# A bias moved ahead of the first values, a late normalization, earlier transposes, and more zero matmuls at the start of a sliding-window attention and gated MLP kernel

## The chip, the cores and the metric

The kernel runs on one core of a Trainium2 chip. The metric is the device time of one execution in microseconds (us). Each execution also lists its span (first to last instruction; here always 1.7 to 1.8 us less than the time) and the mean granted clock of TensorE, the share of full speed that the profiler recorded. At a mean clock of 0.998 or more, the executions of the kernel before lay between 342.41 and 343.31 us, so they agree within 0.3%.

Engine names in the profile: PE is TensorE, PEld its weight loads, DVE is VectorE, ACT is ScalarE, POOL is GpSimd, SP is SyncE.

## The reference

```python
# shortened
def _attn_ref(q, k, v):            # q, k, v: (8, 8, 576, 64), float32
    scores = scale * q @ k^T
    mask = (rel >= 0) & (rel < 64) # causal, window of 64
    attn = softmax(where(mask, scores, -1e9))
    return attn @ v

def _moe_ref(x, w_gate, w_val, w_out):   # x: (4608, 512), d_ff 1536
    return (maximum(x @ w_gate, 0) * (x @ w_val)) @ w_out
# the attention output, heads joined, is x
```

## The kernel before

The attention is cut in 24 units of 192 query rows with all 8 heads. Two units fill one tile of 384 rows, on which the MLP works. A unit goes through: scores (`u_st`, PE, into "st" in PSUM, where the kernel keeps all its matmul results: "st", "pv", "h", "op"), exp (`u_exp`, ACT, "p"), for units from 2 on a multiplication with the band mask (`u_mask`, DVE), values and row sums (`u_pv`, PE, "pv"), copy of the values (`u_copy`, ACT, "xv"), 32x32 transposes of the sums (`u_sum`, DVE, "sT"), reciprocal and transpose back (`u_back`, DVE, "rT", "rs"), product (`u_norm`, DVE, "xt"). Units 0 and 1 have no mask multiplication: a bias of 0 or -30000 is laid into PSUM by matmuls with the identity (`u_bias`) and the scores add to it.

The MLP's hidden layer makes, for 128 of the 1536 columns at a time, a gate product and a value product "h" on PE, a relu on ACT ("r_sb") and a product on DVE ("g_sb", called a gate below). Then the output matmuls "op" run over g_sb.

All this is woven into one order of instructions by a program clock: `W.at(t, fn)` puts `fn` into the order at program time `t`. Moving a number moves an instruction in the order of its engine, and adds no work.

```python
    def heat(n, to, start=True):
        for _ in range(n):
            nc.tensor.matmul(to, zero[:, 0:128], zero[:, 0:to.shape[1]], ...)   # adds zeros
    ...
    def plan_batch(b, load, trans):          # one batch: transposes of k (2), q (2) at times trans
        ...
    def plan_unit(u, T, exp=0.8, mask=1.5, pv=3.9, copy=(4.7, 6.0), norm=(4.8, 6.1, 7.4, 8.7), gap=0.6):
        W.at(T, lambda: u_st(u))
        ...                                   # v_load; u_exp and u_mask, group by group; u_copy
        W.at(T + pv, lambda: u_pv(u))
        for t, fn in zip(norm, (lambda: u_sum(u, 1), lambda: u_sum(u, 0), lambda: u_back(u), lambda: u_norm(u))):
            W.at(T + t, fn)
    ...
        plan_batch(1, None, (37.5, 39.0, 40.4, 41.8))
    ...
        W.at(5.3, lambda: u_bias(0))
        W.at(5.4, lambda: heat(10, units[0]["spare"], False))
        W.at(8.7, lambda: u_st(0, (0,)))
        W.at(9.5, lambda: heat(8, units[0]["spare"], False))
        W.at(11.0, lambda: u_st(0, (1,)))
        ...                                   # exps and copies of unit 0, exps of unit 1
        W.at(11.4, lambda: u_pv(0, (0, 1)))
        W.at(11.45, lambda: u_bias(1, (2, 3)))
        W.at(11.5, lambda: u_pv(0, (2, 3)))
        W.at(11.6, lambda: u_bias(1, (0, 1)))
        W.at(11.7, lambda: u_st(1))
    ...
        fast = 0.8, 1.5, 3.9, (4.1, 5.3), (4.2, 5.4, 6.4, 7.5), 0.5
        plan_unit(2, 24.0, *fast)
        plan_unit(3, 42.5, *fast)
    ...
        W.advance(13.7)
        ready(1)
        hidden(0, 0, U, 0, 4, 4)              # tile 0, rows of unit 0, first 4 column blocks
        ready(2)
        hidden(0, U, TT, 0, 4, 4)             # rows of unit 1
        hidden(0, 0, TT, 4, NF, 4)            # all rows, the other 8 blocks
        output_by_rows(0)
        ready(3)
        hidden(1, 0, U)                       # tile 1 begins
```

The softmax here doesn't subtract the row's maximum and nothing guards it: scores larger than these inputs give would overflow.

## Time and profile before

| | before |
|---|---|
| time, median of 3 | 342.76 us (342.64 to 342.87) |
| the profiled execution | time 344.84 us, span 343.1 us, mean clock 0.995 |
| PE busy | 332.7 us, 97% of the span |
| DVE, ACT busy | 251.5 us, 186.7 us |

The page's line of busy time by engine:

```profile
PE 332.7 (97%) x2950; PEld 201.2 (59%) x2950; DVE 251.5 (73%) x452; ACT 186.7 (54%) x383; POOL 65.7 (19%) x99
```

With PE at 97% the question is where the other 10 us lie. The prediction shows the rest of the profile before. How its lines are read: in a timeline, the first number is the start in us, the second the time until the group's last instruction ended, then engine, source line, operation, out<-in, shapes and count; in brackets stands how long the engine had been idle before and what ended that idle time. In a table by windows, PE's busy time is the first number after the window's length, and the granted clock stands third from the end. The prediction's stalls are measured from start to start, which gives more than the recorded idle time (1.33 us against 0.76 at the end of tile 0).

The prediction's replay leans on one more thing in this profile: ACT's copies of unit 0's values and DVE's transposes of its sums, which both read "pv", take turns. The copies start at 13.04 us, after 0.42 us for the transposes, and at 15.02; the next transposes at 15.37, behind that copy; the last copy at 16.05, after 0.71 us for them.

### The profile page before, as it was taken

The page shows a single profiled execution, that of the slowest core. Times are in us where ns is not written, and L with a number is a line of the kernel's source. Part 1 is how long each engine was busy: PE and PEld are TensorE (multiplying, and loading weights), DVE is VectorE, ACT ScalarE, POOL GpSimd, SP SyncE. Part 2 cuts the span into 40 slices and gives each one's busy share as a digit, 9 for nine tenths or more (in the row PEclk, how much of TensorE's full clock was granted, in tenths as well). Part 3 has the DMA queues.
Part 4 walks back from the last instruction along what each step waited for, and adds up shares of the span by engine and source line. Part 5 has one row for each costly group of instructions (what it writes and reads, how often), then busy time and mean ns, then how long its engine had stood idle before and what let it go on. Part 6 is the DMA issues. An engine that isn't in the chain of part 4 may idle for free.

```text
span 343.1 us, 7364 instructions
## 1 busy us (share of the span) xinstructions
PE 332.7 (97%) x2950; PEld 201.2 (59%) x2950; DVE 251.5 (73%) x452; ACT 186.7 (54%) x383; POOL 65.7 (19%) x99
## 2 busy tenths in 40 slices
PE   8789999999999999999999999999999999999996
PEld 4476477956646556555555655654664664664653
DVE  5587948998898775797888873878968974875430
ACT  4547157645737546556565565564664663763322
POOL 8723421420122211220120410420120200000000
PEclk9899999999999999999999999999999999999999
DMA  8999998790361941961352962874306401001002
GB/s 214 176 206 196 201 167 150 87 178 31 25 84 42 166 58 63 158 74 63 23 48 77 116 80 92 89 100 105 25 5 119 33 2 71 22 2 62 31 2 93
DMA packets 59666, 30.29 MB, mean 88 GB/s; under 512 B 46064, under 2 KB 51056, under 8 KB 59632
## 3 DMA queue, kind: packets, MB, share of 16 engines
q0 software_dynamic: 53872, 19.21, 52.4%
q1 hardware_dynamic: 5616, 10.55, 8.3%
q8 instruction: 23, 0.38, 0.4%
q14 instruction: 11, 0.09, 0.1%
q10 hardware_dynamic: 144, 0.07, 0.1%
HBM read 39.58 MB, written 9.44 MB: 143 GB/s over the span
## 4 chain that ended last, share of the span: by engine, by line
PE 80%; DVE 11%; issue 4%; DMA 2%; POOL 1%; ACT 1%; ACTq 0%; DVEq 0%; POOLq 0%
PE h L412 48%; PE op L426 21%; PE pv L305 6%; DVE sT L335 3%; PE st L246 3%; DVE g_sb L400 2%; DMA v<-in_v_dram 2%; DVE qT L184 2%; DVE xt L350 1%; DVE rs L344 1%; DVE p L266 1%; DVE kT L184 1%; PE op L458 1%; PE pv L287 1%; PE st L206 1%
## 5 line engine op out<-in xcount | busy, mean ns | idle before, releaser
L400 DVE TENSOR_TENSOR g_sb<-r_sb,h 128x384 f16<-128x384 f32 x144 | 78.3, 549 | 54.0 <-PE h L412 45.8
L412 PE MATMUL h<-xt,wg 128*128 128x384 f16 (+1 forms) x640 | 116.5, 310 | 0.7 <-DVE xt L350 0.7
L412 PE MATMUL h<-xt,wv 128*128 128x384 f16 (+1 forms) x640 | 116.6, 310 | 0.2 <-ACT r_sb L397 0.2
L397 ACT ACTIVATE r_sb<-h 128x384 f32<-128x384 f32 x144 | 71.2, 496 | 51.3 <-PE h L412 43.1
L426 PE MATMUL op<-wo,g_sb 128*128 128x512 f16 x420 | 93.3, 379 | 0.5 <-DVE g_sb L400 0.5
L412 PEld LDWEIGHTS <-wg 128*128 128x128 f16 x640 | 59.3, 98 | 34.7 <-DVE xt L350 1.4
L412 PEld LDWEIGHTS <-wv 128*128 128x128 f16 x640 | 59.7, 98 | 32.0 <-issue 0.5
L192 POOL DMA_DIRECT2D v<-in_v_dram x48 | 40.4, 846 | 189.5 <-PE pv L305 170.1
L426 PEld LDWEIGHTS <-g_sb 128*128 128x128 f16 x420 | 40.9, 98 | 48.8 <-issue 1.1
L335 DVE STREAM_TRANSPOSE sT<-pv 64x384 f32<-64x384 f32 x88 | 51.1, 580 | 11.4 <-PE pv L305 9.8
L260 ACT ACTIVATE p<-st 128x512 f16<-128x512 f32 x92 | 49.9, 604 | 11.6 <-PE st L246 11.4
L433 ACT COPY o_sb<-op 128x512 f32<-128x512 f32 x35 | 20.5, 586 | 61.1 <-PE op L426 61.0
L323 ACT COPY xv<-pv 64x384 f32<-64x384 f32 x88 | 41.7, 474 | 18.3 <-DVE sT L335 8.5
L266 DVE TENSOR_TENSOR p<-p,mask 128x512 f16<-128x512 f16 x88 | 34.2, 420 | 6.5 <-ACT p L260 5.9
L305 PE MATMUL pv<-p,v 128*128 128x128 f16 x352 | 24.1, 219 | 0.4 <-DVE p L266 0.4
L344 DVE STREAM_TRANSPOSE rs<-rT 128x768 f32<-128x768 f32 x24 | 23.5, 979 | 0.8
L305 PEld LDWEIGHTS <-v 128*128 128x128 f16 x352 | 21.6, 98 | 3.7 <-issue 0.9
L350 DVE TENSOR_TENSOR xt<-xv,rs 128x768 f16<-128x768 f32 x24 | 22.7, 947 | 0.7
L184 DVE STREAM_TRANSPOSE kT<-k 128x576 f32<-128x576 f32 (+1 forms) x18 | 19.8, 1119 | 1.9 <-ACT k L177 1.8
L184 DVE STREAM_TRANSPOSE qT<-q 128x576 f32<-128x576 f32 x16 | 19.0, 1239 | 0.9 <-DMA q<-in_q_dram 0.8
L246 PE MATMUL st<-qT,kT 32*128 32x128 f16 x768 | 16.1, 215 | 2.2 <-DVE qT L184 2.2
L246 PEld LDWEIGHTS <-kT 32*128 32x128 f16 x768 | 11.5, 92 | 10.5 <-issue 10.5
(46 smaller groups left out, 80.3 us busy)
## 6 DMA issues: line engine op xcount, KB each, us to landing
out_dram<-o_sb SPq DMA_DIRECT2D x35, 256.0 KB, 2.0
v<-in_v_dram POOLq DMA_DIRECT2D x38, 128.0 KB, 4.0
q<-in_q_dram POOLq DMA_DIRECT2D x16, 288.0 KB, 8.3
k<-in_k_dram POOLq DMA_DIRECT2D x14, 288.0 KB, 6.4
wg<-in_moe_w_gate_dram POOLq DMA_DIRECT2D x3, 512.0 KB, 11.2
wv<-in_moe_w_val_dram POOLq DMA_DIRECT2D x3, 512.0 KB, 13.0
wo<-in_moe_w_out_dram POOLq DMA_DIRECT2D x3, 512.0 KB, 16.3
k<-in_k_dram SPq DMA_DIRECT2D x2, 576.0 KB, 4.0
```

What stands on the lines that cost most here:

```text
L184: nc.vector.transpose(dst.rearrange("p (i j) -> p j i", i=32)[:, j0:j1], src[:, j0:j1])
L192: nc.gpsimd.dma_start(v16[p0:128, w, :, 0:64], v[b, :, k0 + p0:k0 + 128].rearrange("h p d -> p h d"))
L246: nc.tensor.matmul(d["st"][hh][g][:, c:c + 128], kT[rows, hh, ks + 128 * w:ks + 128 * w + 128, dh], qT[rows, hh, ks + 64 * w:ks + 64 * w + ...
L260: nc.scalar.activation(d["p"][g].rearrange("p h c -> p (h c)"), d["st"][0][g], ACT.Exp, scale=scale)
L266: nc.vector.tensor_tensor(p, p, mask.rearrange("p w c -> p (w c)")[:, None, :].to_broadcast([128, 2, 256]), MUL)
L305: nc.tensor.matmul(d["pv"][c % 2][:, c // 2, e, 64 * w:64 * w + 128], v16[:, w, 128 * h - 64 * e:128 * h - 64 * e + 128], d["p"][h % G][:, ...
L323: nc.scalar.copy(d["xs"][rows, n::2], d["pv"][n][rows, :, e, 0:U])
L335: nc.vector.transpose(to[64 * e:64 * e + 64, half::2], d["pv"][half][64 - 64 * e:128 - 64 * e, :, e, 0:U])
L397: nc.scalar.activation(part(r_sb), part(h1), ACT.Relu)
L400: nc.vector.tensor_tensor(g_sb[:, f:f + w, c0:c1], part(r_sb), part(h2), MUL)
L412: nc.tensor.matmul(h[:, b * n:b * n + n], wt[:, c, (f + b) * 128:(f + b) * 128 + 128], xt[:, c, c0:c1], start=(c == 0), stop=(c == NC - 1))
L426: nc.tensor.matmul(op, g_sb[:, f, bass.ds(sub * 128, 128)], wo[:, f], start=(f == 0), stop=(f == NF - 1))
```

## The change

Three things are intended. At the start, PE should not stand idle while it waits for the q transpose and the v transfer: four more zero matmuls, and the first half of unit 1's bias before the values. At the end of tile 0, the gates should not stand in DVE's order behind unit 2's normalization. And the last q transpose of batch 1 should not stand behind the first gate of tile 1.

```diff
-        plan_batch(1, None, (37.5, 39.0, 40.4, 41.8))
+        plan_batch(1, None, (37.0, 37.8, 39.4, 40.8))
...
-        W.at(5.4, lambda: heat(10, units[0]["spare"], False))
+        W.at(5.4, lambda: heat(11, units[0]["spare"], False))
...
-        W.at(9.5, lambda: heat(8, units[0]["spare"], False))
+        W.at(9.5, lambda: heat(11, units[0]["spare"], False))
...
-        W.at(11.45, lambda: u_bias(1, (2, 3)))
+        W.at(11.35, lambda: u_bias(1, (2, 3)))
...
-        plan_unit(2, 24.0, *fast)
+        plan_unit(2, 23.0, 0.8, 1.5, 3.9, (4.7, 6.0), (4.8, 7.4, 11.2, 11.3), 0.6)
```

## The prediction

> **What bounds the kernel now.** I read the page first: TensorE (PE) is busy for 332.7 us of a 343.1 us span, so only some 10 us can be gained anywhere by reordering, and 2% (6.9 us) would take two thirds of that. The chain of waits says the same (80% of it is PE). So I asked where PE is not working, with the busy time by stage. The windows are cut at the places where the records of the granted clock change (5.32, 12.15, 15.56 us) and at the starts of the blocks of matmuls.
>
> ```profile
> 5.32:8.74 3.42, 3.01 (x37) 2.17 (x35) 2.62 (x5) 1.52 (x3) 3.42 (x5) 1.00 1.30 186
> 8.74:12.15 3.41, 1.83 (x43) 1.21 (x33) 2.06 (x3) 1.95 (x7) 3.06 (x5) 1.00 2.72 134
> 12.15:15.56 3.41, 3.41 (x34) 1.71 (x34) 1.36 (x4) 1.43 (x5) 2.31 (x3) 0.50 1.24 203
> 15.56:18.97 3.41, 2.17 (x65) 1.68 (x64) 3.23 (x7) 2.38 (x5) 1.27 (x2) 1.00 1.24 206
> ...
> 24.96:37.32 12.36, 12.13 (x114) 7.54 (x113) 9.59 (x22) 7.84 (x16) 4.07 (x6) 1.00 1.36 201
> 37.32:45.94 8.62, 8.09 (x38) 3.51 (x36) 6.32 (x8) 1.17 (x2) 4.63 (x7) 1.00 2.30 168
> 45.94:49.81 3.87, 3.50 (x66) 3.10 (x64) 2.11 (x3) 1.57 (x3) 0.17 (x1) 1.00 2.39 159
> ```
>
> The columns are the window, its length, busy time of PE, weight loads, VectorE (DVE), ScalarE (ACT), GpSimd, then the granted clock, DMA share and GB/s. See row three: PE is busy without a gap, but at a granted clock of 0.50. The window before it had PE busy for 1.83 of 3.41 us (54%); the one after had 2.17 (64%) and the clock was not lowered after it. After 75 us PE has no stage of this size left: 99.80 of 100 us between 100 and 200, and again between 200 and 300. Everything is decided before 50 us. There the timeline of PE shows what it waits for:
>
> ```profile
> 8.86 1.05 PE L213 MATMUL st<-zero 128*128 128x256 f16 x8
> 10.97 0.41 PE L246 MATMUL st<-qT,kT 32*128 32x128 f16 x16 [1.06 <-DVE qT L184]
> 11.31 0.25 PE L287 MATMUL pv<-p,v 128*64 128x128 f16 x2
> 12.08 0.29 PE L287 MATMUL pv<-p,v 128*64 128x128 f16 x2 [0.52 <-DMA v<-in_v_dram]
> ...
> 12.95 1.03 PE L206 MATMUL st<-bias,ident 128*128 128x512 f16 x2
> 13.91 0.42 PE L287 MATMUL pv<-p,v 128*64 128x128 f16 x4
> ```
>
> Two holes, 1.06 us before the second scores and 0.52 us before the values, make the 54%. The bias of unit 1 (0.96 us at half clock, 12.95 to 13.91) stands between the two halves of unit 0's values. Later, at the end of tile 0:
>
> ```profile
> 36.67 0.81 PE L412 MATMUL h<-xt,wv 128*128 128x384 f16 x4 [0.23 <-ACT r_sb L397]
> 38.57 1.02 PE L426 MATMUL op<-wo,g_sb 128*128 128x512 f16 x4 [0.22 <-DVE g_sb L400]
> 38.44 0.94 DVE L350 TENSOR_TENSOR xt<-xv,rs 128x768 f16<-128x768 f32 x1
> 39.30 1.01 DVE L400 TENSOR_TENSOR g_sb<-r_sb,h 128x384 f16<-128x384 f32 x2
> ```
>
> The gates (g_sb) that free PSUM for the output wait on DVE behind unit 2's four transposes, reciprocal, transpose back and normalization.
>
> [...]
>
> **The change part by part.** The built order shows one more zero matmul before the first scores, three more before the second, the bias pair of unit 1 before unit 0's values, scores of unit 2 four matmuls earlier and its values four matmuls earlier, and on DVE the reciprocal, transpose and normalization of unit 2 after the last gate of tile 0. From the transposes of batch 1 on only their place against the first gate of tile 1 differs.
>
> *Zeros.* Four of about 0.11 us[...]. The first hole (0.41 us) and the second (1.06 us) hold them: no cost on the path. The second hole shrinks to some 0.74 us.
>
> *Bias.* Two matmuls of 512 columns, 0.43 us at full clock, go into the 0.52 us before the v transfer lands (12.04 us in the trace). Then that hole is about 0.1 us. PE in 8.74 to 12.15 is busy 1.83 + 0.32 + 0.42 = 2.57 us, 75%[...]. So I expect full clock from 12.15.
>
> *First stage, replayed.* v lands as before, 12.08. Values of channels 0 and 1 end their issue at 12.47 instead of 12.80 (0.11 instead of 0.21 us per four). The exps end at 12.62, so the second half of the values starts at 12.68 (before: 13.91) and has channel 2 by about 13.1. ACT copies channels 0 and 1 from 12.9 to 13.6[...], channel 2 13.63 to 13.95, DVE transposes two to 14.63, ACT copies channel 3 to 14.98. The exps of unit 1 then start at 15.04 instead of 16.43: **1.39 us earlier**. PE's bias and scores (to 14.2) are no longer on this path, ACT is. From there to the first matmul of tile 0 (19.08 before) all durations stay: 17.69. Weights landed at 15.54, 18.17, 20.76, 23.29, 25.80, 28.80 us; they are used at 17.7, 19.0, 23.6, 26.2, 29.4, 32.9, so none becomes a wait.
>
> *End of tile 0.* From 24.96 to 45.94 are 20.98 us. Work by start-to-start spacing: 64 matmuls of 384 columns at 0.1625 = 10.40, scores 0.57, values 0.90, 36 output matmuls at 0.216 = 7.78: 19.65. Stalls 1.33 us (recorded idle 0.76[...]). Replayed with the new DVE order, the gates 8 to 11 end at about 34.3, 36.0, 36.4, 36.9 against outputs that ask for them at 35.5, 36.3, 37.2: **1.33 us gained**. Unit 2's xt is done by about 39.2, tile 1 asks for it at 43.2. Its values start at 30.65, v landed 29.95: it fits.
>
> *Scores of unit 3.* They stood 0.49 us (48.97 expected, 49.46 seen) for the last q transpose, which stood on DVE behind the first gate of tile 1, at 47.68. Now it comes before that gate; q landed at 43.41, transposed by 44.8, scores at about 46: **0.49 us gained**.
>
> Sum: 1.39 + 1.33 + 0.49 = 3.2 us; 342.76 − 3.2 = 339.6.
>
> **The rivals.** (1) *The clock falls one window later.* With PE faster and ACT the bound, PE stands from about 14.25 to 15.6; in 12.15 to 15.56 it is busy only some 2.1 us[...]. Then 15.56 to 18.97 runs at half, and the first 1.28 us of tile 0 before 18.97 do half their work, a loss of some 0.65 plus 0.2 in the values: 340.4. I give it two in five. (2) *The clock falls as before*[...]. The moved bias still lets the second half of the values start at 12.95, but bias and scores of unit 1 run at half until 15.75: exps at 15.85, gain 0.6 in place of 1.39: 340.4 too. One in six. (3) *A transfer becomes the bound*: slack is 0.7 us for v of unit 2, 0.8 for the second weights and 1.1 for q of batch 1; each could return some 0.3 us. (4) *The delayed normalization makes tile 1 wait*: 4 us of slack speak against it. (5) *DVE bound at 60 to 70 us* (busy 98%) gives time back: its order there is unchanged and follows PE, so hardly.
>
> **Range and chances.** Between 339.6 (all three gains) and 340.4 (a clock rival), I say 339.9. [...]three runs before lay within 0.23 us; gains mis-sized by half a microsecond each give 339.0 to 341.2. To be faster by over 2% it would have to lie under 335.9: the 6.9 us are more than PE's whole idle time from 5 to 60 us (5.0, by the busy times of windows of 5 us) and half of the half-clock stretch (1.7) together; to be slower, over 349.6, of which there is no sign. So within 2%, 0.98.
>
> **What would show it.** Right: clock 1.00 from 12.15 to 15.56; bias at about 11.3 and second values at about 12.7; exps of unit 1 at 15.0; first tile-0 matmul at 17.7; no wait of outputs for gates and none of relu before 37 us; scores of unit 3 without a wait; the first matmul of tile 1 about 2.7 us earlier; from 60 us on a constant offset of about 3.2. Wrong: a row at 0.50 clock anywhere after 12 us; a DMA named as releaser of PE at tile 0; more recorded PE idle between 20 and 60 us than the 1.8 of before (40 less 38.19).

## The result

The changed kernel took 340.80 us (median of 4, 340.72 to 340.91) against 342.75 us (342.64 to 342.87), beside each other. The ratio is 0.9943, with a 95% interval of 0.9926 to 0.9960. A ratio is the mean time of one kernel's executions over that of the other's of the same rounds, so it is not quite the ratio of the medians. By this the kernel is 1.95 us faster, which is within 2%, and the time lies in the predicted range.

The profiled execution after spans 339.0 us, its mean clock is 0.999. That is 4.1 us less than the profiled execution before, but the times differ by 1.95 us only. One of the two profiles does not stand for the timed executions.

PE's timeline of the changed kernel, the start and the end of tile 0:

```profile
10.64 0.41 PE L246 MATMUL st<-qT,kT 32*128 32x128 f16 x16
10.99 0.61 PE L206 MATMUL st<-bias,ident 128*128 128x512 f16 x2
11.53 0.30 PE L287 MATMUL pv<-p,v 128*64 128x128 f16 x4
...
14.79 0.22 PE L287 MATMUL pv<-p,v 128*64 128x128 f16 x1 [0.93 <-ACT p L260]
...
16.80 1.49 PE L412 MATMUL h<-xt,wg 128*128 128x192 f16 x16
...
34.64 7.93 PE L426 MATMUL op<-wo,g_sb 128*128 128x512 f16 x36
...
45.15 0.64 PE L246 MATMUL st<-qT,kT 32*128 32x128 f16 x32
...
55.67 0.83 PE L412 MATMUL h<-xt,wg 128*128 128x192 f16 x8 [0.26 <-DVE xt L350]
```

Two lines of DVE and one of ACT from the same execution:

```profile
14.13 2.07 ACT L260 ACTIVATE p<-st 128x512 f16<-128x512 f32 x4
...
34.75 1.48 DVE L400 TENSOR_TENSOR g_sb<-r_sb,h 128x384 f16<-128x384 f32 x3
...
37.50 0.96 DVE L350 TENSOR_TENSOR xt<-xv,rs 128x768 f16<-128x768 f32 x1
```

The hole before the second scores is gone, and the bias fills the wait for v. The 36 output matmuls run in one row without a wait, and the 32 score matmuls of unit 3 in one row too; the last three gates of tile 0 now come before unit 2's product on DVE. One hole has grown: PE stands 0.93 us before the values of unit 1, for ACT's exps (0.69 us in the first profile). The same in the table by windows, cut at the starts of the stages:

```profile
22.67:34.64 11.97, 11.97 (x114) 7.54 (x113) 8.97 (x20) 7.83 (x16) 3.73 (x6) 1.00 1.37 200
34.64:42.41 7.77, 7.77 (x38) 3.52 (x36) 7.26 (x10) 1.17 (x2) 4.02 (x5) 1.00 1.29 202
42.41:45.72 3.31, 3.31 (x66) 3.05 (x64) 2.30 (x4) 1.57 (x3) 1.45 (x4) 1.00 3.74 125
```

PE is busy through all three: 11.97 of 11.97 us, 7.77 of 7.77, 3.31 of 3.31. Before, these stages were 12.36, 8.62 and 3.87 us long. That is 0.39, 0.85 and 0.56 us less, 1.80 us in sum.

### The profile page after: what moved, and what is told of

Same layout as the page of the kernel before. It is cut to its first block, busy times and chain, and to the rows that moved or that the text cites. A ratio compares the mean times of both kernels' runs of the same rounds, so it can differ in the third digit from the quotient of the medians.

```text
span 339.0 us, 7368 instructions
## 1 busy us (share of the span) xinstructions
PE 331.4 (98%) x2954; PEld 201.0 (59%) x2954; DVE 251.9 (74%) x452; ACT 186.1 (55%) x383; POOL 65.6 (19%) x99
## 4 chain that ended last, share of the span: by engine, by line
PE 85%; DVE 10%; issue 3%; ACT 1%; ACTq 0%
PE h L412 50%; PE op L426 21%; PE pv L305 6%; PE st L246 3%; DVE sT L335 3%; PE st L213 2%; DVE g_sb L400 2%; DVE qT L184 1%; DVE xt L350 1%; DVE p L266 1%; DVE kT L184 1%; PE op L458 1%; ACT p L260 1%; DVE rs L344 1%; PE st L206 1%
```

## The experiments

**Theory A**: the half-clock stretch from 12.15 to 15.56 us, on which the first step of the prediction rests, belongs to that one profiled execution. In the timed executions before, PE had its full clock, the start is bounded by ACT's copies and exps, and the gain is the end of tile 0 and the scores of unit 3. **Rival B**: the stretch belongs to each execution of the kernel before, and the start gave most of the gain. There were twelve runs, all correct, in three calls of four, each in five rounds beside the kernel before. Two calls ran on chip 13 and the middle one on chip 8, so a run is compared with the kernel before of its own call.

### The kernel before, again

No edit.

> The kernel before, unchanged, to see its granted clock in the timed executions. Theory A (the half-clock window of the first profile is an accident of that one execution, and the timed ones ran at full clock): spans near 341.0 us, mean clock 0.999 or more in nearly all executions, time 342.75. Rival B (the window at half clock belongs to every execution of this kernel): spans near 343.1 us at a mean clock of 0.995.

Measured: 342.75 us median of 6. Five of them have spans of 340.8 to 341.1 us at a mean clock of 1.000; one has 342.8 us at 0.994. All eleven executions of the kernel before in the same call have 0.999 or 1.000. Theory A holds on the clock, and B falls. This profile fell in a usual execution. PE's timeline of it, and ACT's exps of unit 1:

```profile
10.78 0.41 PE L246 MATMUL st<-qT,kT 32*128 32x128 f16 x16 [0.52 <-DVE qT L184]
11.12 0.33 PE L287 MATMUL pv<-p,v 128*64 128x128 f16 x4
...
11.71 0.61 PE L206 MATMUL st<-bias,ident 128*128 128x512 f16 x2
12.25 0.30 PE L287 MATMUL pv<-p,v 128*64 128x128 f16 x4
...
14.18 2.07 ACT L260 ACTIVATE p<-st 128x512 f16<-128x512 f32 x4
...
14.83 0.22 PE L287 MATMUL pv<-p,v 128*64 128x128 f16 x1 [0.83 <-ACT p L260]
...
16.84 1.49 PE L412 MATMUL h<-xt,wg 128*128 128x192 f16 x16
```

The hole before the second scores is 0.52 us, not 1.06; v landed at 11.16 us in place of 12.04, so there is no wait for it at all; and PE then stands 0.83 us for the exps. The exps start at 14.18 us, against 14.13 in the changed kernel. By the profile's chain of waits the bias between the values (0.54 us, from 11.78) is on the path to the exps here, and in the changed kernel it is still on it, now ahead of the values (0.54 us, from 11.06). From the second scores to the exps it takes 3.40 us here and 3.49 there: with v landed early, the move gains nothing. This is the profile to compare with:

| start of (us) | before, first profile | before, again | after | after less again |
|---|---|---|---|---|
| first matmul of tile 0 | 19.08 | 16.84 | 16.80 | -0.04 |
| output of tile 0 | 37.32 | 35.07 | 34.64 | -0.43 |
| tile 1 | 45.94 | 43.69 | 42.41 | -1.28 |
| h after the scores of unit 3 | 49.81 | 47.56 | 45.72 | -1.84 |
| second half of tile 1 | 59.77 | 57.52 | 55.67 | -1.85 |
| span | 343.1 | 340.8 | 339.0 | -1.8 |

The first row has to be read with care. In the five profiles at full clock that have the bias in its old place, tile 0 starts at 16.69 to 17.48 us, by when v lands: 5.68 or 5.69 us after v in four of them (v at 11.16, 11.48, 11.51 and 11.80 us), and in the fifth (v at 10.86) 6.04 us after the second scores.

### The start part alone

```diff
-        W.at(5.4, lambda: heat(10, units[0]["spare"], False))
+        W.at(5.4, lambda: heat(11, units[0]["spare"], False))
-        W.at(9.5, lambda: heat(8, units[0]["spare"], False))
+        W.at(9.5, lambda: heat(11, units[0]["spare"], False))
-        W.at(11.45, lambda: u_bias(1, (2, 3)))
+        W.at(11.35, lambda: u_bias(1, (2, 3)))
```

> Only the first part of the change: the zeros and the moved bias. Theory A: at full clock ScalarE's chain of copies and exps starts where it did, so 0 to 0.3 us faster than before. Rival B: the start is where most was gained, so 1.2 to 2.0 us faster.

Measured: 343.36 us median of 6, ratio 1.0019 (1.0006 to 1.0033). No gain: rival B falls a second time. Three executions at a clock of 0.998 or more took 342.49 to 343.15 us, as the kernel before; the other three, at 0.993 to 0.994, took 343.57 to 343.98. In this profile, at full clock, PE stood 0.29 us for the second weights (wv, a transfer) at 18.55 us, which is the prediction's third rival. It cost nothing there: the next stage started at 19.99 us, without its usual wait of 0.41 us for unit 1's xt (20.02 in the changed kernel).

### The tile-0 part alone

```diff
-        plan_batch(1, None, (37.5, 39.0, 40.4, 41.8))
+        plan_batch(1, None, (37.0, 37.8, 39.4, 40.8))
-        plan_unit(2, 24.0, *fast)
+        plan_unit(2, 23.0, 0.8, 1.5, 3.9, (4.7, 6.0), (4.8, 7.4, 11.2, 11.3), 0.6)
```

> Only the second part: unit 2's scores earlier, its reciprocals and normalization after the last gate of tile 0, and the transposes of batch 1 ahead. Theory A: 1.33 + 0.49 = 1.8 us faster than before, nearly the whole 1.95 of the change. Rival B: 0.5 us or less.

Measured: 341.08 us median of 5 (340.94 to 341.28), ratio 0.9951 (0.9939 to 0.9963), that is 1.7 us. This part is the gain, as theory A has it, within the intervals.

### Without the eight zeros between the scores

```diff
-        W.at(9.5, lambda: heat(8, units[0]["spare"], False))
+        W.at(9.5, lambda: heat(0, units[0]["spare"], False))
```

> The kernel before without its eight zero matmuls between the two groups of scores, so that the hole there grows from 1.06 to some 2 us and provokes the half clock. If idle time within a window lowers the clock: a stretch at 0.50 of 3.41 us in most executions, spans up by 1.5 to 2.3 us where it is there, times in two groups. If the zeros do nothing for the clock: the time of before, within 0.2 us.

Measured: 344.04 us median of 6, ratio 1.0027 (1.0006 to 1.0047), in two groups, as the first case of the expectation says. Four executions at 0.995 span 342.2 to 343.0 us, two at 1.000 span 340.7 and 340.9. The profile fell in the first group. Its windows, cut where the clock changes:

```profile
8.90:12.31 3.41, 0.93 (x35) 0.69 (x30) 1.95 (x3) 2.08 (x8) 2.91 (x5) 1.00 2.62 135
12.31:15.72 3.41, 3.41 (x36) 1.40 (x34) 1.89 (x5) 1.31 (x5) 2.29 (x3) 0.50 1.25 209
```

PE was busy for 27% of the window before the half clock. So the zeros that were there before are worth having: without them four of six executions span 1.3 to 2.3 us more than the other two, and the kernel that has them is at 0.995 or less in 2 of 41. Where there is no half clock, taking them away costs nothing (340.7 and 340.9 us of span, against 340.8 to 341.1 in the five usual executions of the kernel before, again).

### Only the normalization of unit 2 late

```diff
-        plan_unit(2, 24.0, *fast)
+        plan_unit(2, 24.0, 0.8, 1.5, 3.9, (4.1, 5.3), (4.2, 5.4, 12.2, 12.3), 0.5)
```

> The kernel before with only unit 2's reciprocals, transpose back and normalization moved behind the last gate of tile 0; PE's and ScalarE's order stay. The two stalls of the output matmuls for gates go (start to start 1.25 and 1.33 us in place of 0.86 each: 0.86 us), ScalarE's late relu stays (0.4 us): 0.85 us faster than before. If the waits only move elsewhere: 0.3 us or less.

Measured: 342.00 us median of 5 against 342.79, ratio 0.9975 (0.9963 to 0.9988), 0.86 us: the expected size. PE's timeline has the output in one row, and keeps ScalarE's late relu and the scores' wait:

```profile
35.07 0.81 PE L412 MATMUL h<-xt,wv 128*128 128x384 f16 x4 [0.23 <-ACT r_sb L397]
35.72 7.93 PE L426 MATMUL op<-wo,g_sb 128*128 128x512 f16 x36
...
47.01 0.41 PE L246 MATMUL st<-qT,kT 32*128 32x128 f16 x16 [0.38 <-DVE qT L184]
```

### Only the transposes of batch 1 ahead

```diff
-        plan_batch(1, None, (37.5, 39.0, 40.4, 41.8))
+        plan_batch(1, None, (37.0, 37.8, 39.4, 40.8))
```

> The kernel before with only the times of batch 1's transposes changed; in the built order that is the last q transpose ahead of the first gate of tile 1 and nothing else. The scores of unit 3 lose their stand of 0.49 us (0.39 recorded): 0.5 us faster. If q's landing is the true limit there: 0.1 us or less.

Measured: 342.36 us median of 5 against 342.79, ratio 0.9985 (0.9973 to 0.9998), 0.5 us: the expected size, with an interval that nearly reaches 1. The timeline shows the other half of the picture, scores in one row and the stalls of the output kept:

```profile
36.17 1.02 PE L426 MATMUL op<-wo,g_sb 128*128 128x512 f16 x4 [0.23 <-DVE g_sb L400]
37.50 6.20 PE L426 MATMUL op<-wo,g_sb 128*128 128x512 f16 x28 [0.30 <-DVE g_sb L400]
...
46.28 0.64 PE L246 MATMUL st<-qT,kT 32*128 32x128 f16 x32
```

The two parts give 1.36 us together and the whole tile-0 part 1.7. By the timelines what is left is the relu's wait (0.39 us from start to start): both of these runs keep it, and it is gone in the tile-0 part, where unit 2's scores, values and copies are moved as well. No run moved these alone, and the 0.3 us is within the intervals of the three runs, so this last piece is read from the traces and not measured.

### The changed kernel, again

No edit.

> The changed kernel, unchanged, for more executions beside the kernel before on one chip. If the parts simply add (start part alone 0 at full clock, tile-0 part alone 1.6 us): 341.0 us at full clock, 1.6 to 1.95 under before. If the start part lowers the clock one window later in some executions, as three of its six alone did (clock 0.993, 343.6 to 344.0 us): some executions at 341.8 to 342.3 us with a mean clock near 0.993.

Measured: 341.23 us median of 5 (340.67 to 341.35), all at a clock of 1.000; ratio 0.9948 (0.9936 to 0.9961). The parts add, and none of its nine executions had a low clock.

### Unit 3 earlier

To the changed kernel, aimed at the 0.26 us wait for xt at 55.67 us:

```diff
-        plan_unit(3, 42.5, *fast)
+        plan_unit(3, 42.2, *fast)
```

> The changed kernel with unit 3's scores and values each four matmuls (0.33 us) earlier, aimed at the wait that is left at tile 1's second half (0.26 us recorded, 0.6 from start to start) for unit 3's xt. If that wait follows the values: 0.3 us faster than the changed kernel of this call. If the q transfer (landed 42.85) or VectorE bounds the scores: the same time, within 0.15 us.

Measured: 341.32 us median of 5, ratio to the kernel before 0.9961 (0.9947 to 0.9974): no gain over the changed kernel. The time is that of the second expectation, but for neither of its reasons. The wait aimed at is gone, and another stands in its place:

```profile
53.14 0.81 PE L426 MATMUL op<-wo,g_sb 128*128 128x512 f16 x3 [0.52 <-ACT r_sb L397]
```

With the values earlier, both copies of values stand ahead of two relus in ACT's order, and the output waits 0.52 us for the relu. Two of its five executions were at a clock of 0.995 (341.79 and 342.02 us).

### Only the zeros

```diff
-        W.at(5.4, lambda: heat(10, units[0]["spare"], False))
+        W.at(5.4, lambda: heat(11, units[0]["spare"], False))
-        W.at(9.5, lambda: heat(8, units[0]["spare"], False))
+        W.at(9.5, lambda: heat(11, units[0]["spare"], False))
```

> The kernel before with only the four extra zero matmuls. They stand in holes of PE, so at full clock the time of before within 0.15 us. If they keep the clock up, no execution with a mean clock under 0.997; if they do not matter, about one in ten, as of the kernel before (2 of 31 so far).

Measured: 342.97 us median of 5 against 342.84, ratio 1.0001 (0.9987 to 1.0014), no execution under 0.999. The extra zeros cost nothing; that they keep the clock up five executions cannot show, when the kernel before has a low clock in 2 of 41.

### Only the bias

```diff
-        W.at(11.45, lambda: u_bias(1, (2, 3)))
+        W.at(11.35, lambda: u_bias(1, (2, 3)))
```

> The kernel before with only unit 1's bias (2, 3) ahead of unit 0's values. If ScalarE's copies and exps bound the start at full clock, PE's earlier work changes nothing: the time of before within 0.2 us at a clock of 0.998 or more. If it brings the clock down one window later: executions at 0.993 and about 1 us longer, as in three of six of the first start-part run.

Measured: 342.76 us median of 6, ratio 1.0005 (0.9992 to 1.0018). At full clock 342.57 to 342.77, the time of before; two of six at 0.993 took 343.54 and 343.92. Both lines of the expectation came true.

### The start part alone, once more

The same edit as in the first start-part run.

> The start part alone once more, to tell whether its three slow executions of six were the kernel's own or chance. Its own: again two or more of six at a clock near 0.993, median 0.4 us or more over before. Chance: one at most, and the time of before within 0.2 us.

Measured: 342.69 us median of 6, ratio 1.0004 (0.9988 to 1.0019). One of six was slow: 344.38 us at 0.993, and the profile fell in it. So the three of six in the first run were in part chance; the median of the start part is that of the kernel before. The windows of this profile, cut at the clock's changes and at the window before them, and PE's timeline:

```profile
13.82:17.23 3.41, 1.92 (x56) 1.37 (x56) 3.06 (x7) 2.53 (x7) 1.63 (x2) 1.00 1.24 207
17.23:20.65 3.42, 3.42 (x32) 3.10 (x30) 2.88 (x7) 1.57 (x5) 0.74 (x1) 0.50 1.24 206
```

```profile
15.65 0.22 PE L287 MATMUL pv<-p,v 128*64 128x128 f16 x1 [0.95 <-ACT p L260]
...
17.98 2.74 PE L412 MATMUL h<-xt,wg 128*128 128x192 f16 x16
20.52 1.55 PE L412 MATMUL h<-xt,wv 128*128 128x192 f16 x16
```

Here the half clock comes one window later. The hole before the values of unit 1 and the two short ones behind it left PE busy for 1.92 of 3.41 us (56%), and tile 0's first sixteen matmuls then took from 17.98 to 20.52, 2.54 us in place of 1.32. This is the prediction's first rival, seen. In the changed kernel's own profile the window from 13.77 to 17.18 us has PE busy for 1.93 us (57%), and its clock was 1.00 in the window after it: the recorded busy time does not separate the two. The kernel before, again, has 2.03 us (60%) in its window from 13.86 to 17.27, and kept 1.00 too. Where to place these two windows is an estimate: steps of 3.41 us from the first record of full clock (at 6.94 and 7.03 us). The half clock lasted 3.41 or 3.42 us in the three profiles that have one in their first 25 us, and in the first of them it began 6.83 us, two such lengths, after that record (5.32 to 12.15).

The first record of full clock lay at 5.32 and 7.03 us in two profiles of the same kernel, the one before. What decides whether a half clock comes (341.0 or 342.8 us of span in one set of six of that kernel) is not shown: the three profiles that have one are also the three of fourteen in which v landed latest (12.01 to 12.09 us, the others 10.86 to 11.80).

Counting executions at a mean clock of 0.995 or less (for the first four timed executions of the kernel before no clock is listed; their times are those of full clock): 2 of 41 of the kernel before and 0 of 20 of the four other kernels that have its eight zeros or more and the bias in its old place; 8 of 37 of the five kernels that have the bias moved (the changed kernel 0 of 9 of these, the copy on VectorE 0 of 5, the others 8 of 23). Moving the bias takes PE's idle time out of one place and adds it to the hole before unit 1's values (0.83 us before, 0.93 to 0.95 after), which suggests that it makes the later half clock likelier. The count was made after the fact and is uneven among those five, so this is argued and not shown.

### One copy moved to VectorE

To the changed kernel, in `u_copy`:

```diff
-            nc.scalar.copy(d["xs"][:, c], d["pv"][c][:, 0])
+            (nc.vector.tensor_copy if (u, c) == (0, 3) else nc.scalar.copy)(d["xs"][:, c], d["pv"][c][:, 0])
```

> The changed kernel with the copy of unit 0's last channels moved from ScalarE to VectorE, so that ScalarE's exps of unit 1 need not wait for it. If ScalarE's chain bounds the start: exps start at 13.9 in place of 14.13, the first tile-0 matmul at 16.55 in place of 16.80, and the whole 0.2 us faster than the changed kernel, unless the second weights (landed 17.7 to 18.5) take it back as a wait for a transfer. If PE bounds it: no shift.

Measured: 341.05 us median of 5, ratio to the kernel before 0.9948 (0.9936 to 0.9960), the same as the changed kernel. ScalarE's timeline has the exps behind the scores, at 14.02 us, but tile 0's second start is no earlier:

```profile
14.02 2.06 ACT L260 ACTIVATE p<-st 128x512 f16<-128x512 f32 x4 [0.68 <-PE st L246]
...
16.67 1.50 PE L412 MATMUL h<-xt,wg 128*128 128x192 f16 x16
...
20.17 1.49 PE L412 MATMUL h<-xt,wg 128*128 128x192 f16 x16 [0.68 <-DVE xt L350]
```

The start gained about 0.1 us at 16.67 (16.80 in the changed kernel). Counted from the second scores, which came later here (10.78 us, 10.64 in the changed kernel), it gained 0.27 us (5.89 in place of 6.16), the expected size: in the changed order ScalarE's copies and exps are on the path of this stage. DVE's extra copy set its order back (unit 0's product starts at 15.64 us in place of 15.34) and took the gain: PE waits 0.68 us for unit 1's xt, where it waited 0.41, and starts at 20.17 in place of 20.02.

No version beats the changed kernel beyond the noise. The tile-0 part alone equals it within the intervals (0.9951 against 0.9943 and 0.9948).

## Why the prediction was right or wrong

The time (340.8 us) was within the range, 0.9 us above the point (339.9 us), and the class was right. The sum of the steps was not: it says 3.2 us, and 1.95 were measured. Its sums and its readings of the lines hold when they are done again; what failed is the execution that they were read from, and with it the replay of the start.

- **Zeros: right.** They cost nothing (zeros alone: ratio 1.0001).
- **First stage, 1.39 us: wrong, and this is the step that failed.** It took the half clock of the profiled execution for the clock of the timed ones. That the change would bring full clock from 12.15 us was an estimate from two windows of that one profile, 54% busy before the half clock and 64% before a full one; no run showed a rule behind them (56% and 57% went different ways, above). Against the kernel before at full clock the first matmul of tile 0 is 0.04 us earlier, the start part alone is no faster in either of its two runs (1.0019 and 1.0004), and the bias alone is not either (1.0005). In the old place at full clock tile 0 starts 5.68 us after v, so with v landing at 12.04, as in the first profile, the unchanged kernel would reach it at 17.72 us by this estimate. The prediction gave 17.69 for the changed one: what it counted as the gain of this step was the half clock, which costs 1.36 us by the same estimate (19.08 less 17.72).
  The idea of the moved bias was not wrong in itself. In the five profiles at full clock that have it moved (without the copy on VectorE), tile 0 starts 6.15 us after the second scores, whether v landed at 11.13 or 11.52 us: it does hide a late v. Applied to the landings in the five profiles with the old order, that is worth from -0.1 to 0.3 us, an estimate that the timed runs cannot tell from nothing. For the landings of the first profile it would be some 0.4 us (17.72 less 17.32, by the 5.28 us from v to tile 0 in the changed kernel, where v landed as the bias ended). The replay missed this part: it took 2.96 us from the first values after v to the exps (12.08 to 15.04), where the changed kernel took 2.60 (11.53 to 14.13). It said that "PE's bias and scores (to 14.2) are no longer on this path, ACT is"; PE's first bias pair is still on it.
  The sign that was missed is plain: the profiled execution took 344.84 us, the timed ones 342.64 to 342.87.
- **End of tile 0, 1.33 us: the mechanism right, the size nearly.** From the first 384-column matmul to tile 1 the profiles at full clock differ by 1.24 us (0.39 before the output, 0.85 in it). Measured alone, the late normalization gave 0.86 us. The relu's wait, which the prediction counted in the same sum, is gone where the scores, values and copies are moved too.
- **Scores of unit 3, 0.49 us: right.** The stage is 0.56 us shorter, and the transposes alone gave 0.5 us.
- **Rivals.** The clock one window later was seen in a trace, with the start part alone; in the changed kernel it was in none of nine executions. The clock as before: not seen after the change. A transfer as the bound: not in the changed kernel's two profiles; the nearest were 0.29 us for the second weights (the start part alone, at no cost) and, in the run with unit 3 earlier, 0.26 us for the v transfer of unit 2, which landed at 30.41 us. Late normalization and DVE at 60 to 70 us: no wait came of them; from 45.7 us on the offset is constant at 1.84 to 1.85.

So the range held because I put the point 0.3 us above the full sum for the clock rivals and left room for mis-sized gains. To that extent it was luck: the room was meant for other causes than a gain that did not exist, and the time came 0.4 us below the upper end. The centre was off by the wrong baseline: with 0.04 in place of 1.39, the steps as they stood give 1.86 us, or 340.9.

## What to carry to other kernels

Before a change is costed on a profile, compare the profiled execution's own time with the timed ones; if it is 0.6% off, as here, find what differs (here a stretch at half clock, and a transfer that landed later) and leave that out. A wait that one engine fills with other work is only worth something if it shortens the path that ends the stage, and if the wait is there in the usual executions. Here v had landed by 11.16 us in the usual profile, and the moved bias lay on the path in its new place as in its old one. In an order that is worked front to back, work that frees a buffer for the bound engine goes ahead of work whose result is asked for later: that was worth 0.86 us for two moved numbers.
